# A routed expert layer behind cross attention: the list of surely positive units cut from 512 to 448 rows, the opening by head groups, and two inserted steps moved

## The chip, the cores and the metric

The kernel runs on one core of a Trainium2 chip. The metric is the device time of one execution in microseconds (us). TensorE (PE) multiplies, with its weight loads on a row of their own (PEld); VectorE (DVE) and ScalarE (ACT) do elementwise work; GpSimd (POOL) issues the indirect transfers; SyncE (SP) issues most of the others. In a profile, a wait is put down to whatever released it.

## The reference

```python
scores = scale * np.matmul(x, state.transpose(0, 1, 3, 2))      # x: 8 x 8 x 512 x 64, state: 8 x 8 x 32 x 64
a = softmax(scores);  xread = np.matmul(a, state)               # every token reads the states
a2 = softmax(scale * np.matmul(state, x.transpose(0, 1, 3, 2)))
sread = np.matmul(a2, x)                                        # every state reads the tokens
x = concat([xread, sread], axis=2) -> (8 * 544, 512)
expert_idx = argmax(x @ w_gate);  gate_w = softmax(...)[expert_idx]
out = gate_w * (relu(x @ w1[expert]) @ w2[expert])              # 8 experts, 512 -> 1024 -> 512, all float32
```

## The kernel before, in words

All 512 tokens of a batch go, as a rule, to one expert, which is guessed from the sum of the batch's states. A repair branch at the end computes anew every pair of batch and expert for which that does not hold, or whose lists overflowed; it is skipped when the count is zero.

Since `xread` is a weighted sum of states, the first layer of a batch is written `aT` (attention weights, 256 x 512 tokens) times `G` (states times w1, 256 x 1024 units). Each of the 1024 hidden units of a batch is put in one of three classes from mean and spread of its column of `G`: surely over zero for every token (then relu does nothing and the unit is linear), surely below zero (it is dropped), or unsure. `lists(b)` ranks them, and POOL scatters the columns to `g_dram`: rows 0 to `CAPP`-1 hold the sure ones, the next `CAPU` rows the unsure ones. `fetch(b)` reads the lists back, `gather(b, n)` gets the matching rows of w2 by indirect DMAs, one per block of 128 rows, and `mask(b)` zeroes unused rows.

`batch(b, insert)` then computes a batch from the lists. `pgu`: transposes of the unsure block. `pm`: for both halves g of the states, the sure rows times their rows of w2 (`NP` = 4 blocks of 128 rows, one matmul of 128x512 each), copied to `M` by ACT, so that the linear part needs only `aT` times `M`. `phu`: the unsure units, with relu, to `hu` (one block of 128 rows, one of 64). `py`: for each of 4 token blocks `aT` times `M` (two matmuls), the 128 unsure rows (one matmul), and the 64 last ones: two token blocks are done as a pair, each with a lhsT of 64 partitions, one on the lower and one on the upper half of the array. `store` scales by the gate and writes out. Batch 0 is done in full by `in_full`.

Everything for later batches is written into this work by hand. `batch` calls `insert()` 13 times: after `pgu`, four times during `pm`, after each of the two `phu`, and three times in each half of `py`. Each call takes the next entry of a plan, a string of letters; each letter runs the next step of a generator: T (`fronts`: transposes of x, scores, softmax), B (`backs`: five steps a batch, namely turn of the exponents a2, bound, state read, logits, `pcnt` = count of tokens by expert), S (`lists`), F (`fetch`, then two gathers), M (mask), R (`tokens`: sorting the 256 state rows by expert and three rounds of 128 rows through the experts' weights). Every engine executes its instructions in the order written here. PSUM tiles other than the scores come from one pool of 6 banks (`bank`).

An fp32 matmul of 128x512 stands in the trace as two records.

The opening: `load_x(0)` brings the 8 heads of batch 0 in two DMAs (heads 0 to 3, 4 to 7); `turn_x` transposes them, `scores` computes the scores of all heads in two groups (even and odd heads), `shifted`, `exp0`, `norm_read` and `turn_read` make the softmax for one group at a time, `turn_states` and `guess(1, B)` prepare states and experts of batches 1 to 7, and `states_w1` makes the first half of batch 0's `G`.

Of the kernel before, what the change touches and what calls it, by code (L numbers as in the profile page):

```python
# [20 lines left out]
def kernel(  # L21
# [52 lines left out]

    CAPP, CAPU = 512, 192
    YB = 4
    NP, NU = CAPP // 128, 2
    GW = 2 * 128 + 1
# [32 lines left out]
    def load_x(b, q):  # L111
        x_nat[b] = att.tile([128, H, NC, D], FP32, tag="x", bufs=2, name="x_nat")
        for h in (ts(0, 4), ts(1, 4)):
            q.dma_start(out=x_nat[b][:, h].rearrange("p h c d -> p h (c d)"),
                        in_=x[b, h].rearrange("h (p c) d -> p h (c d)", c=NC))

# [60 lines left out]
    nn = const.tile([128, B, 2], FP32)  # L177
    dve.memset(nn[:], 0.0)
    more = const.tile([128, NT], FP32)
# [90 lines left out]

    def scores(xT, st):

        for g in range(2):
            for q in range(4):
                for c in range(2):
                    pe.matmul(pa[ts(q, 32), c, g], lhsT=st[ts(c, 64), 2 * q + g, :], rhs=xT[ts(c, 64), 2 * q + g],
                              start=True, stop=True, skip_group_check=True)
# [26 lines left out]
    def new_aT():  # L304
        return ffn.tile([128, 2, NC, 4, 32], FP32, tag="aT", bufs=4, name="aT")
# [40 lines left out]
    def back(b):  # L346
# [25 lines left out]
        for g in range(2):  # L372
            for c in range(NC):
                for q in range(4):
                    pe.matmul(pw[ts(q, 32), g], lhsT=a2T[:, g, c, ts(q, 32)], rhs=x_nat[b][:, 2 * q + g, c, :],
                              start=(c == 0), stop=(c == NC - 1), skip_group_check=True)
# [113 lines left out]
    def store_batch(b):  # L490
        rows = out[ds(b * SO, S)].rearrange("(p c) f -> p c f", c=NC)

        def store(c, py):
            y = ffn.tile([128, DM], FP32, tag="y", bufs=YB, name="y")
            if b == B - 1 and c == NC - 1:
                dve.tensor_scalar(y[:], py[:], gw[:, NC * b + c, :], None, ALU.mult)
            else:
                act.activation(y[:], py[:], AF.Copy, scale=gw[:, NC * b + c, :])
            no_dep((act if b == B - 1 and c == NC - 2 else sp).dma_start(out=rows[:, c], in_=y[:]))
        return store  # L500
# [3 lines left out]
    def lists(b):  # L504
# [40 lines left out]
        dve.tensor_copy(out=nn[:, b], in_=pr[:, NFC:2 * NFC + 2:NFC + 1])  # L545
        fits, at_l, at_u, off_u = small("s_f"), small("s_l"), small("s_u"), small("s_o", 1)
        dve.scalar_tensor_tensor(fits[:], pr[:, 0:NFC], float(CAPP), lin, ALU.is_lt, ALU.mult)
        dve.scalar_tensor_tensor(at_l[:], pr[:, 0:NFC], -float(FAR), fits[:], ALU.add, ALU.mult)
        dve.tensor_scalar(off_u[:], nn[:, b, 0:1], -1.0, float(CAPP - FAR), ALU.mult, ALU.add)
        dve.scalar_tensor_tensor(at_u[:], pr[:, NFC + 1:2 * NFC + 1], off_u[:], und, ALU.add, ALU.mult)  # L550
# [11 lines left out]
    def fetch(b):  # L562

        t = gps[b] = ffn.tile([128, NP + NU, GW], FP32, tag="gp", bufs=2, name="gp")
        gp.dma_start(out=t[:, 0:NP + 1], in_=g_dram[0:CAPP + 128].rearrange("(j p) k -> p j k", p=128))
        for u in range(2):
            gp.dma_start(out=t[ts(u, 64), NP + 1], in_=g_dram[ds(CAPP + 128, 64)])
        w2cs[b] = []
# [11 lines left out]
    def mask(b):  # L580

        t = gps[b]
        mk = ffn.tile([128, NP + NU], FP32, tag="mk", bufs=2, name="mk")
        dve.tensor_scalar(mk[:, 0:NP], slot_p[:], nn[:, b, 0:1], None, ALU.is_lt)
        dve.scalar_tensor_tensor(mk[:, NP:], slot_u[:], nn[:, b, 0:1], nn[:, b, 1:2].to_broadcast([128, NU]),
                                 ALU.add, ALU.is_lt)
        for j in [NP, NP + 1, *range(NP)]:
            dve.tensor_scalar(t[:, j, 0:256], t[:, j, 0:256], mk[:, j:j + 1], None, ALU.mult)
# [3 lines left out]
    def batch(b, insert):  # L592
# [7 lines left out]
        insert()  # L600
        M = ffn.tile([128, 2, DM], FP32, tag="M", name="M")
        for g in range(2):
            pm = bank(name="pm")
            for j in range(NP):
                pe.matmul(pm[:], lhsT=t[:, j, ts(g, 128)], rhs=w2c[j][:], start=(j == 0), stop=(j == NP - 1))
                if j % 2:
                    insert()
            act.copy(M[:, g, :], pm[:])
        summed[0] = b
# [15 lines left out]
        for c0 in range(0, NC, 2):  # L625
            py = [bank(name="py") for _ in range(2)]
            for i in range(2):
                for g in range(2):
                    pe.matmul(py[i][:], lhsT=tokens_of(a)[:, g, ts(c0 + i, 128)], rhs=M[:, g, :],
                              start=(g == 0), stop=False)  # L630
                pe.matmul(py[i][:], lhsT=hu[0][:, ts(c0 + i, 128)], rhs=w2c[NP][:], start=False, stop=False)
                insert()
            for i in range(2):
                pe.matmul(py[i][:], lhsT=hu[1][ts(i, 64), ts(c0 // 2, 128)], rhs=w2c[NP + 1][ts(i, 64)],
                          start=False, stop=True)
            for i in range(2):
                store(c0 + i, py[i])
            insert()
# [159 lines left out]
    sx0 = new_sx()  # L798
    aTs[0] = new_aT()
    dve.tensor_copy(out=std[:, 0:2, 1], in_=std[:, 0:2, 0])  # L800
    turn_states(0, 2, copy_dve)
# [27 lines left out]
    off = const.tile([128, 1], FP32)  # L829
    gp.memset(off[:], -1.0 / NS)  # L830
    U128 = const.tile([128, 128], BF16)

# [3 lines left out]
    def late_constants():  # L836
        clear()
        yield
        dve.tensor_scalar(U128[:], colf[:], iota_p[:, 0:1], None, ALU.is_gt)
        tmp = const.tile([128, 1], FP32)  # L840
        quad = const.tile([128, 1], FP32)
        dve.tensor_scalar(quad[:], iota_p[:], 32.0, None, ALU.is_ge)
        for q in (64.0, 96.0):
            dve.scalar_tensor_tensor(quad[:], iota_p[:], q, quad[:], ALU.is_ge, ALU.add)
        dve.tensor_scalar(tmp[:], quad[:], float(SO - NS), iota_p[:, 0:1], ALU.mult, ALU.add)
        for t in range(NT):
            dve.tensor_scalar(tok_s[:, t:t + 1], tmp[:], float(4 * t * SO + S), None, ALU.add)
        dve.tensor_copy(out=slot_u[:, 0:1], in_=iota_p[:])
        dve.tensor_scalar(tmp[:], iota_p[:], 64.0, -64.0, ALU.is_ge, ALU.mult)
        dve.scalar_tensor_tensor(slot_u[:, 1:2], iota_p[:], 128.0, tmp[:], ALU.add, ALU.add)  # L850
        yield

# [83 lines left out]
    def count_left():  # L936
# [7 lines left out]
        tmp8 = const.tile([128, B], FP32)  # L944
        dve.tensor_tensor(tmp8[:], nn[:, :, 1], nn[:, :, 0], ALU.subtract)
        dve.tensor_scalar(over[:, :, 0], nn[:, :, 0], float(CAPP), None, ALU.is_gt)
        dve.scalar_tensor_tensor(over[:, :, 0], tmp8[:], float(CAPU), over[:, :, 0], ALU.is_gt, ALU.max)
        dve.tensor_tensor(others[:], others[:], over[:].to_broadcast([128, B, E]), ALU.max)
# [21 lines left out]
    with tc.If(number(rest_i[0:1, 0:1], B * E + NT * NR * 3) > 0):  # L970
# [4 lines left out]
        with tc.If(number(n_i[0:1, 0:1], B * E) > 0):  # L975
# [8 lines left out]
            with tc.For_i(0, n_pairs, 1):  # L984
# [20 lines left out]
                for h in range(H):  # L1005
                    sp.dma_start(out=xn[:, h].rearrange("p c d -> p (c d)"),
                                 in_=x[ds(bs, 1), h].rearrange("o (p c) d -> p (o c d)", c=NC))
# [69 lines left out]
```

## Time and profile before

| | us |
|---|---|
| median of 3 runs | 394.77 (393.68 to 395.79) |
| the profiled execution | 391.03 |
| its span, first to last instruction | 389.2 |
| PE busy in it | 359.8 (92%) |
| DVE, ACT, POOL busy | 189.5, 131.1, 123.3 |
| DMA | 92.65 MB, mean 238 GB/s |

Matmuls are pipelined and the ends of their records are modelled, so their starts say more than their durations: from start to start a record of 128x512 fp32 takes 0.43 us here.

### The profile page before, as it was taken

Reading aid. Unit: us, or ns where it says so; the run is one execution under the profiler, and the core shown is the slowest. Engines: PE = TensorE matmul, PEld = TensorE weight load, DVE = VectorE, ACT = ScalarE, POOL = GpSimd, SP = SyncE. Lnnn points to the kernel's source line nnn. Section 1 sums busy time; section 2 is a strip of 40 time slices with the busy share of each in tenths; the row PEclk is TensorE's granted clock in tenths of the full one; section 3 lists DMA queues with packets and bytes.
Section 4 is the critical chain, followed back from the end, with each engine's and each line's share of the span. In section 5 each row is a group of like instructions: output and inputs, shape, how many; then the busy total and the mean of one; then the engine's idle time right before and its main releaser. Section 6 shows DMA issues by size and latency. Waiting matters only on the chain. (4 is left out here: it accounts for less than half of the span.)

```text
span 389.2 us, 7854 instructions
## 1 busy us (share of the span) xinstructions
PE 359.8 (92%) x2660; PEld 166.3 (43%) x2660; DVE 189.5 (49%) x614; ACT 131.1 (34%) x249; POOL 123.3 (32%) x146
## 2 busy tenths in 40 slices
PE   5599999999799898999997799999999999999992
PEld 4344553645444364455441335333443443432330
DVE  3857678784588167967740223533733364000100
ACT  2464824623622444263334124104541032211010
POOL 2000017277317533643273321073510747000000
PEclk9899999999999899999998899999999999999997
DMA  7979992973563655243899999599996356979952
GB/s 167 376 235 278 242 365 84 318 231 106 159 195 109 196 158 178 96 133 82 281 367 334 346 395 390 198 322 262 329 331 207 128 161 199 314 238 340 389 200 85
DMA packets 50765, 92.65 MB, mean 238 GB/s; under 512 B 8007, under 2 KB 18258, under 8 KB 50720
## 3 DMA queue, kind: packets, MB, share of 16 engines
q1 hardware_dynamic: 41920, 69.95, 54.7%
q0 software_dynamic: 8128, 21.86, 17.9%
q8 instruction: 23, 0.38, 0.4%
q10 hardware_dynamic: 672, 0.28, 0.3%
q14 instruction: 22, 0.18, 0.1%
HBM read 83.40 MB, written 20.42 MB: 267 GB/s over the span
## 5 line engine op out<-in xcount | busy, mean ns | idle before, releaser
L51 POOL DMA_INDIRECT g_dram<-gt,to x56 | 56.9, 1016 | 132.2 <-DMA x_nat<-in_x_dram 52.9
L51 POOL DMA_INDIRECT w2c<-in_moe_w_dram,gp x42 | 44.0, 1048 | 58.3 <-DMA gp<-g_dram 31.4
L51 PE MATMUL py<-M,aT 128*128 128x512 f32 x112 | 54.2, 607 | 0.0
L51 PE MATMUL pm<-w2c,gp 128*128 128x512 f32 x112 | 53.1, 609 | 0.0
L51 PE MATMUL py<-w2c,hu 128*128 128x512 f32 (+1 forms) x112 | 44.7, 634 | 0.0
L51 ACT ACTIVATE y<-py,gw 128x512 f32<-128x512 f32 x31 | 20.0, 686 | 58.1 <-PE py L51 28.6
L51 PE MATMUL pgh<-s,sxT 128*32 128x512 f32 x192 | 28.3, 636 | 3.2 <-issue 2.8
L51 PEld LDWEIGHTS py<-M,aT 128*128 128x128 f32 x112 | 19.8, 189 | 26.7 <-issue 23.2
L51 DVE BATCH_NORM_STATS2 bn<-gt 128x6 f32<-128x256 f32 x56 | 20.2, 416 | 20.3 <-ACT gt L51 16.7
L51 PEld LDWEIGHTS pm<-w2c,gp 128*128 128x128 f32 x112 | 20.3, 195 | 20.8 <-issue 18.9
L51 DVE COPY G<-pG 128x512 f32<-128x512 f32 x14 | 9.6, 689 | 39.8 <-PE pG L51 23.8
L51 PEld LDWEIGHTS py<-w2c,hu 128*128 128x128 f32 (+1 forms) x112 | 15.1, 192 | 22.2 <-issue 22.1
L51 PE MATMUL pgy<-s,shT 128*32 128x512 f32 x192 | 23.7, 596 | 0.0
L51 PE MATMUL pG<-w1t,stT 64*32 64x512 f32 x256 | 21.2, 622 | 1.7 <-issue 1.6
L51 PE MATMUL py<-s,s 128*128 128x512 f32 x48 | 22.6, 603 | 0.0
L51 ACT COPY xT<-pxT 128x512 f32<-128x512 f32 x30 | 16.3, 604 | 15.5 <-PE pxT L51 13.1
L51 DVE COPY shT<-pth 128x512 f32<-128x512 f32 x3 | 2.1, 689 | 39.8 <-PE pth L51 39.8
L51 PE MATMUL phu<-aT,Gu 128*64 128x256 f32 (+1 forms) x84 | 20.7, 461 | 0.0
L51 ACT COPY gt<-pgt 128x512 f32<-128x512 f32 x28 | 15.9, 599 | 13.2 <-PE pgt L51 9.1
L51 POOL DMA_INDIRECT out_dram<-ys,xg x3 | 3.0, 991 | 52.2 <-DVE ys L51 49.5
L51 ACT ACTIVATE a<-pa,nm 128x512 f32<-128x512 f32 x16 | 10.9, 686 | 22.4 <-DVE nm L51 20.4
L51 PE MATMUL pxT<-ident,x_nat 128*128 128x128 f32 x128 | 17.8, 294 | 0.2 <-PE ph L51 0.2
(207 smaller groups left out, 487.2 us busy)
## 6 DMA issues: line engine op xcount, KB each, us to landing
s<-in_moe_w_dram SPq DMA_DIRECT2D x144, 256.0 KB
w1t<-in_moe_w_dram SPq DMA_DIRECT2D x7, 2048.0 KB
x_nat<-in_x_dram SPq DMA_DIRECT2D x16, 512.0 KB
out_dram<-y SPq DMA_DIRECT2D x31, 256.0 KB
gp<-g_dram POOLq DMA_DIRECT2D x7, 642.5 KB
ss_dram<-blank SPq DMA_DIRECT2D x8, 257.0 KB
w1t<-in_moe_w_dram SPq DMA_DIRECT2D x2, 1024.0 KB
s<-in_moe_w_dram SPq DMA_DIRECT2D x2, 768.0 KB
```

Of the source, the lines that this page charges most:

```text
L51: ins = getattr(self.engine, name)(*args, **kw)
```

## The change

`CAPP` goes from 512 to 448, so that the lists take 640 rows in place of 704. Sure units from rank 448 on are no longer dropped: the unsure list begins right behind row 447, and the surplus sure units are put there and treated as unsure. The fourth block of sure rows (384 to 447) is fetched twice, onto partitions 0 to 63 and 64 to 127, and its matmuls for g = 0 and g = 1 use one half of the array each. `fetch` issues four DMAs in place of three. Both `pm` banks are taken at once, and both copies to `M` come after the pair.

In `py`, the second half begins with its pair of 64-row matmuls and stores each block as it is done; the last block of the last batch is scaled half by ACT, half by DVE, and written by two DMAs on two queues.

`load_x` brings even heads first, then odd ones. In the opening, scores, shift and exponentials go group by group, the copy of the states and `turn_states` stand elsewhere, and `guess(1, B)` comes last. Two plan entries differ: the first B step of batch 3 (turn of exponents) moves from the last entry of batch 0 to the first of batch 1, and the `pcnt` of batch 4 from `BTR` to the entry behind it. The 13 calls of `insert` per batch stay; in `pm` they are three after 2, 4 and 6 matmuls and one after the pair and the copies.

```diff
-    CAPP, CAPU = 512, 192
+    CAPP, CAPU = 448, 192
-    NP, NU = CAPP // 128, 2
+    NP, NU = 4, 2
...
-        for h in (ts(0, 4), ts(1, 4)):
-            q.dma_start(out=x_nat[b][:, h].rearrange("p h c d -> p h (c d)"),
-                        in_=x[b, h].rearrange("h (p c) d -> p h (c d)", c=NC))
+        for g in range(2):
+            q.dma_start(out=x_nat[b][:, ts(g, 4)].rearrange("p h c d -> p h (c d)"),
+                        in_=x[b, g:H:2].rearrange("h (p c) d -> p h (c d)", c=NC))
...
             if b == B - 1 and c == NC - 1:
-                dve.tensor_scalar(y[:], py[:], gw[:, NC * b + c, :], None, ALU.mult)
+                act.activation(y[:, 0:256], py[:, 0:256], AF.Copy, scale=gw[:, NC * b + c, :])
+                dve.tensor_scalar(y[:, 256:], py[:, 256:], gw[:, NC * b + c, :], None, ALU.mult)
+                no_dep(act.dma_start(out=rows[:, c, 0:256], in_=y[:, 0:256]))
+                no_dep(sp.dma_start(out=rows[:, c, 256:], in_=y[:, 256:]))
             else:
                 act.activation(y[:], py[:], AF.Copy, scale=gw[:, NC * b + c, :])
-            no_dep((act if b == B - 1 and c == NC - 2 else sp).dma_start(out=rows[:, c], in_=y[:]))
+                no_dep(sp.dma_start(out=rows[:, c], in_=y[:]))
...
-        dve.scalar_tensor_tensor(fits[:], pr[:, 0:NFC], float(CAPP), lin, ALU.is_lt, ALU.mult)
-        dve.scalar_tensor_tensor(at_l[:], pr[:, 0:NFC], -float(FAR), fits[:], ALU.add, ALU.mult)
-        dve.tensor_scalar(off_u[:], nn[:, b, 0:1], -1.0, float(CAPP - FAR), ALU.mult, ALU.add)
+        dve.tensor_scalar(nl[:, b:b + 1], nn[:, b, 0:1], float(CAPP), None, ALU.min)
+        dve.scalar_tensor_tensor(at_l[:], pr[:, 0:NFC], -float(FAR), lin, ALU.add, ALU.mult)
+        dve.tensor_scalar(off_u[:], nl[:, b:b + 1], -1.0, float(CAPP - FAR), ALU.mult, ALU.add)
...
-        gp.dma_start(out=t[:, 0:NP + 1], in_=g_dram[0:CAPP + 128].rearrange("(j p) k -> p j k", p=128))
-        for u in range(2):
-            gp.dma_start(out=t[ts(u, 64), NP + 1], in_=g_dram[ds(CAPP + 128, 64)])
+        gp.dma_start(out=t[:, 0:NP - 1], in_=g_dram[0:384].rearrange("(j p) k -> p j k", p=128))
+        for i in range(2):
+            gp.dma_start(out=t[ts(i, 64), NP - 1::2], in_=g_dram[384:CAPP + CAPU].rearrange("(j p) k -> p j k", p=64)[:, 0::3])
+        gp.dma_start(out=t[:, NP], in_=g_dram[ds(CAPP, 128)])
...
+        pm = [bank(name="pm") for _ in range(2)]
+        for n in range(2 * NP - 2):
+            g, j = n // (NP - 1), n % (NP - 1)
+            pe.matmul(pm[g][:], lhsT=t[:, j, ts(g, 128)], rhs=w2c[j][:], start=(j == 0), stop=False, skip_group_check=True)
+            if n % 2:
+                insert()
         for g in range(2):
-            pm = bank(name="pm")
-            for j in range(NP):
-                pe.matmul(pm[:], lhsT=t[:, j, ts(g, 128)], rhs=w2c[j][:], start=(j == 0), stop=(j == NP - 1))
-                if j % 2:
-                    insert()
-            act.copy(M[:, g, :], pm[:])
+            pe.matmul(pm[g][:], lhsT=t[ts(g, 64), NP - 1, ts(g, 128)], rhs=w2c[NP - 1][ts(g, 64)], start=False, stop=True,
+                      skip_group_check=True)
+        for g in range(2):
+            act.copy(M[:, g, :], pm[g][:])
+        insert()
...
+            def few(start):
+                for i in range(2):
+                    pe.matmul(py[i][:], lhsT=hu[1][ts(i, 64), ts(c0 // 2, 128)], rhs=w2c[NP + 1][ts(i, 64)],
+                              start=start, stop=not start, skip_group_check=True)
+            if c0 > 0:
+                few(True)
...
+                if c0 > 0:
+                    store(c0 + i, py[i])
...
+    act.copy(std[:, 2:, 1], std[:, 2:, 0])
     exp0 = lambda g: act.activation(sx0[:, ts(g, 16)], sx0[:, ts(g, 16)], AF.Exp, bias=0.0, scale=SCALE)
-    scores(xT0, stT[:, 0])
-    shifted(sx0, [0])
-    exp0(0)
-    shifted(sx0, [1])
-    act.copy(std[:, 2:, 1], std[:, 2:, 0])
+    for g in range(2):
+        scores(xT0, stT[:, 0], [g])
+        shifted(sx0, [g])
+        exp0(g)
     turn_states(2, 6, act.copy)
-    turn_states(6, 10, act.copy)
     norm_read(sx0, [0])
-    exp0(1)
-    turn_states(10, 14, act.copy)
-    turn_states(14, 16, act.copy)
     turn_read(sx0, aTs[0], [0])
-    pick = guess(1, B)
-    norm_read(sx0, [1])
-    turn_read(sx0, aTs[0], [1])
...
     states_w1(w1t, stT[:, 0], G, 0, act.copy)
-    pick()
+    norm_read(sx0, [1])
+    turn_read(sx0, aTs[0], [1])
+    turn_states(6, 10, act.copy)
+    turn_states(10, 14, act.copy)
+    turn_states(14, 16, act.copy)
+    guess(1, B)()
...
-        "TGKK,TAT,A,TA,,TST,SBA,SSSS,BBTT,SSAT,TB,T,SBTS,TBST,BSSS,STBF,FSSB,,TT,B,T,,TTMS,SSBS"))
+        "TGKK,TAT,A,TA,,TST,SBA,SSSS,BBTT,SSAT,TB,T,SBTS,TBST,BSSS,STBF,FSSB,,TT,B,T,,TTMS,SSS"))
-        1: "FTFS,,,B,BT,SFBS,BTT,,,R,,MBSS,FSTB",
-        2: "STSS,TB,TF,RR,MFS,RFBS,BTR,,T,,R,TTS,SBTF",
+        1: "BFTFS,,,B,BT,SFBS,BTT,,,R,,MBSS,FSTB",
+        2: "STSS,TB,TF,RR,MFS,RFBS,TR,B,T,,R,TTS,SBTF",
```

More of the change, by code (lines that the diff above doesn't have):

```diff
@@ L177 @@
     nn = const.tile([128, B, 2], FP32)
-    dve.memset(nn[:], 0.0)
+    nl = const.tile([128, B], FP32)
+    for t in (nn, nl):
+        dve.memset(t[:], 0.0)
     more = const.tile([128, NT], FP32)
@@ L269, in new_xT, with scores @@
         return att.tile([128, H, 2, 128], FP32, tag="xt", name="xT")
-    def scores(xT, st):
-        for g in range(2):
+    def scores(xT, st, groups=(0, 1)):
+        for g in groups:
             for q in range(4):
                 for c in range(2):
-                    pe.matmul(pa[ts(q, 32), c, g], lhsT=st[ts(c, 64), 2 * q + g, :], rhs=xT[ts(c, 64), 2 * q + g],
+                    pe.matmul(pa[ts(q, 32), c, g], lhsT=st[ts(c, 64), 2 * q + g, :], rhs=xT[ts(c, 64), 4 * g + q],
                               start=True, stop=True, skip_group_check=True)
@@ L374, in back @@
                 for q in range(4):
-                    pe.matmul(pw[ts(q, 32), g], lhsT=a2T[:, g, c, ts(q, 32)], rhs=x_nat[b][:, 2 * q + g, c, :],
+                    pe.matmul(pw[ts(q, 32), g], lhsT=a2T[:, g, c, ts(q, 32)], rhs=x_nat[b][:, 4 * g + q, c, :],
                               start=(c == 0), stop=(c == NC - 1), skip_group_check=True)
@@ L545, in lists @@
         dve.tensor_copy(out=nn[:, b], in_=pr[:, NFC:2 * NFC + 2:NFC + 1])
-        fits, at_l, at_u, off_u = small("s_f"), small("s_l"), small("s_u"), small("s_o", 1)
-        dve.scalar_tensor_tensor(fits[:], pr[:, 0:NFC], float(CAPP), lin, ALU.is_lt, ALU.mult)
-        dve.scalar_tensor_tensor(at_l[:], pr[:, 0:NFC], -float(FAR), fits[:], ALU.add, ALU.mult)
-        dve.tensor_scalar(off_u[:], nn[:, b, 0:1], -1.0, float(CAPP - FAR), ALU.mult, ALU.add)
+        at_l, at_u, off_u = small("s_l"), small("s_u"), small("s_o", 1)
+        dve.tensor_scalar(nl[:, b:b + 1], nn[:, b, 0:1], float(CAPP), None, ALU.min)
+        dve.scalar_tensor_tensor(at_l[:], pr[:, 0:NFC], -float(FAR), lin, ALU.add, ALU.mult)
+        dve.tensor_scalar(off_u[:], nl[:, b:b + 1], -1.0, float(CAPP - FAR), ALU.mult, ALU.add)
         dve.scalar_tensor_tensor(at_u[:], pr[:, NFC + 1:2 * NFC + 1], off_u[:], und, ALU.add, ALU.mult)
@@ L584, in mask @@
         dve.tensor_scalar(mk[:, 0:NP], slot_p[:], nn[:, b, 0:1], None, ALU.is_lt)
-        dve.scalar_tensor_tensor(mk[:, NP:], slot_u[:], nn[:, b, 0:1], nn[:, b, 1:2].to_broadcast([128, NU]),
+        dve.scalar_tensor_tensor(mk[:, NP:], slot_u[:], nl[:, b:b + 1], nn[:, b, 1:2].to_broadcast([128, NU]),
                                  ALU.add, ALU.is_lt)
@@ L629, in batch @@
                     pe.matmul(py[i][:], lhsT=tokens_of(a)[:, g, ts(c0 + i, 128)], rhs=M[:, g, :],
-                              start=(g == 0), stop=False)
-                pe.matmul(py[i][:], lhsT=hu[0][:, ts(c0 + i, 128)], rhs=w2c[NP][:], start=False, stop=False)
-                insert()
[L633 to L637, printed above, removed]
+                              start=(c0 == 0 and g == 0), stop=False, skip_group_check=True)
+                pe.matmul(py[i][:], lhsT=hu[0][:, ts(c0 + i, 128)], rhs=w2c[NP][:], start=False, stop=c0 > 0,
+                          skip_group_check=True)
+                if c0 > 0:
+                    store(c0 + i, py[i])
+                insert()
+            if c0 == 0:
+                few(False)
+                for i in range(2):
+                    store(c0 + i, py[i])
             insert()
@@ L799 @@
     aTs[0] = new_aT()
+    off = const.tile([128, 1], FP32)
+    gp.memset(off[:], -1.0 / NS)
+    U128 = const.tile([128, 128], BF16)
     dve.tensor_copy(out=std[:, 0:2, 1], in_=std[:, 0:2, 0])
@@ L827 @@
     states_w1(w1t, stT[:, 0], G, 0, act.copy)
-    pick()
-    off = const.tile([128, 1], FP32)
-    gp.memset(off[:], -1.0 / NS)
-    U128 = const.tile([128, 128], BF16)
+    norm_read(sx0, [1])
[4 more added lines that the diff above has]
+    guess(1, B)()
     slot_u = const.tile([128, NU], FP32)
@@ L850, in late_constants @@
         dve.scalar_tensor_tensor(slot_u[:, 1:2], iota_p[:], 128.0, tmp[:], ALU.add, ALU.add)
+        dve.tensor_tensor(slot_p[:, NP - 1:NP], slot_p[:, NP - 1:NP], tmp[:], ALU.add)
         yield
@@ L944, in count_left @@
         tmp8 = const.tile([128, B], FP32)
-        dve.tensor_tensor(tmp8[:], nn[:, :, 1], nn[:, :, 0], ALU.subtract)
-        dve.tensor_scalar(over[:, :, 0], nn[:, :, 0], float(CAPP), None, ALU.is_gt)
-        dve.scalar_tensor_tensor(over[:, :, 0], tmp8[:], float(CAPU), over[:, :, 0], ALU.is_gt, ALU.max)
+        dve.tensor_tensor(tmp8[:], nn[:, :, 1], nl[:], ALU.subtract)
+        dve.tensor_scalar(over[:, :, 0], tmp8[:], float(CAPU), None, ALU.is_gt)
         dve.tensor_tensor(others[:], others[:], over[:].to_broadcast([128, B, E]), ALU.max)
@@ L1005 @@
                 for h in range(H):
-                    sp.dma_start(out=xn[:, h].rearrange("p c d -> p (c d)"),
+                    sp.dma_start(out=xn[:, h % 2 * 4 + h // 2].rearrange("p c d -> p (c d)"),
                                  in_=x[ds(bs, 1), h].rearrange("o (p c) d -> p (o c d)", c=NC))
```

## The prediction, on record before the changed kernel ran

> **What bounds the kernel now.** I read the page's busy times and slices first, then PE's matmuls in order of time, then the opening, SP's queue of the last third, and the places where PE stands still.
>
> ```profile
> PE 359.8 (92%) x2660; PEld 166.3 (43%) x2660; DVE 189.5 (49%) x614; ACT 131.1 (34%) x249; POOL 123.3 (32%) x146
> PE   5599999999799898999997799999999999999992
> PEclk9899999999999899999998899999999999999997
> ```
>
> PE is the bound nearly throughout; 389.2 - 359.8 leaves 29 us idle, and slices of 7 and 8 show where. So a matmul taken from PE's row shortens the run, except where something else is later. Batch 6 shows a `pm` with nothing inserted (timeline of PE; start, length):
>
> ```profile
> 311.42 1.13 PE L51 MATMUL py<-w2c,hu 64*128 64x512 f32 x4
> ...
> 313.43 7.11 PE L51 MATMUL pm<-w2c,gp 128*128 128x512 f32 x16
> 320.37 2.89 PE L51 MATMUL phu<-aT,Gu 128*128 128x512 f32 x12
> ```
>
> From start to start the 16 records take 6.94 us, 0.43 each. The pair of 64-row matmuls (311.42 to the next start at 312.48) takes 1.06 for four records: two run at a time, 2 x 0.43 plus 0.20 for changing the array's form.
>
> The opening (timeline, all engines):
>
> ```profile
> 9.94 0.69 DVE L51 COPY xT<-pxT 128x512 f32<-128x512 f32 x1 [1.01 <-PE pxT L51]
> ...
> 11.79 0.78 DVE L51 STREAM_TRANSPOSE sx<-pa 128x256 f32<-128x256 f32 x2 [1.16 <-PE pa L51]
> ...
> 14.59 0.92 ACT L51 COPY std<-std 128x896 f32<-128x896 f32 x1
> ...
> 15.56 2.22 PE L51 MATMUL pst<-ident,std 128*128 128x128 f32 x14 [3.82 <-ACT std L51]
> ...
> 20.54 0.71 DVE L51 STREAM_TRANSPOSE aT<-sx 128x512 f32<-128x512 f32 x1
> ...
> 21.27 1.98 PE L51 MATMUL ph<-aT,G 128*128 128x512 f32 x4 [0.15 <-ACT G L51]
> ```
>
> DVE's softmax chain runs without a break from 11.79 to 21.25 and releases batch 0's first `ph`; it starts only when all scores are there. PE idles 3.82 us for the copy of the states.
>
> The last third (SP's queue; two stretches: length, busy us of PE, PEld, DVE, ACT, POOL, clock, DMA share, GB/s):
>
> ```profile
> 324.65 0.33 SPq L51 DMA_DIRECT2D xg<-ss_dram  x1
> 326.60 14.18 SPq L51 DMA_DIRECT2D s<-in_moe_w_dram  x15
> 340.88 6.56 SPq L51 DMA_DIRECT2D out_dram<-y  x4
> 347.80 22.50 SPq L51 DMA_DIRECT2D s<-in_moe_w_dram  x33
> ```
>
> ```profile
> 336.00:368.00 32.00, 31.50 (x149) 10.79 (x147) 0.69 (x1) 6.04 (x11) 0.00 (x0) 1.00 0.92 318
> 382.10:389.20 7.10, 0.00 (x0) 0.00 (x0) 0.75 (x1) 0.69 (x1) 0.00 (x0) 0.73 0.21 77
> ```
>
> The third round of state rows needs 48 transfers of 256 KB, which run from 326.60 to about 375 back to back. PE's `pgh` and `pgy` starts are stretched by them: 5.65, 6.67 and 4.87 us for stretches that take 3.57 undisturbed. From 324.65 to 367.94 this stream is the clock, not PE. After the last matmul 7.1 us follow.
>
> Where PE stands still in between (timeline):
>
> ```profile
> 97.70 2.08 POOL L51 DMA_DIRECT2D gp<-g_dram  x3
> ...
> 99.30 0.59 ACT L51 COPY G<-pG 128x512 f32<-128x512 f32 x1 [2.33 <-remote]
> ...
> 99.94 0.66 PE L51 MATMUL pa<-ident,a 128*128 128x128 f32 x4 [2.19 <-ACT G L51]
> ```
>
> ```profile
> 155.21 0.26 PE L51 MATMUL pcnt<-oh,ones_b 128*128 128x8 bf16 x4 [1.31 <-DVE oh L51]
> ```
>
> The first is the turn of exponents that the change moves, the second the `pcnt`. In the first, `pG`'s matmuls started at 93.43 and ran about 1 us, yet ACT, idle from 96.98, began the copy at 99.30, in the middle of a train of POOL transfers. Similar stalls stand at 128.7 to 132.9, 204.5 to 207.4 and 217.8 to 221.9.
>
> **The change part by part.** *The pm cut.* Six matmuls and a pair: 12 x 0.43 + 1.06 = 6.22 in place of 6.94: 0.72 a batch. [...] In `py`, where the entry between the halves has no PE work (batches 1, 2, 3), the two pairs now touch: 0.20 less each. Batches 1 to 5: 5 x 0.72 + 3 x 0.20 = 4.2 us. Batches 6 and 7 lie before or in the weight stream; `xg` at 324.65 hangs on sorting that precedes batch 6's `pm`, so their 1.4 us become longer waits at `pgh`: nothing, at most 1.4.
>
> *The opening.* Scores of group 0 need only the first two copies of xT, so they run while DVE makes the fourth; DVE can start the chain at 9.94 + 0.69 = 10.63 in place of 11.79. The chain's operations stay the same and DVE is never idle in it: 1.1 us earlier at `ph`. Moved steps: ACT's copy of the states now comes before the exponentials (9.68 to 10.6, ACT is idle there; its DMA was issued at 2.31), `turn_states` 6 to 16 and `guess` come behind `states_w1`; their five ACT copies (0.55 or less each) and PE's 2 to 3 us must be done by 20.1. By the rows: exponentials end 15.6, one copy, G's two, three more, 18.6, `guess` and its sums 20.0: just covered, at most 0.5 late. `clear()` drops a DMA of SP's 6 (3.14 us), uncritical. Here the clock decides: from 13.0 to 16.43 PE was busy 0.87 us, and the next 3.41 us ran at a granted clock of 0.54, over small transposes. [...] If that falls on `ph` now, it costs up to 1.7. [...]
>
> *The two moved steps.* `pcnt` waits 1.31 for DVE; one entry later its `oh` is long done, and `prs`, now first, needs an `oh` that DVE finished at 153.37, before `phu` ends. Gain 1.4, from the whole gap behind `phu` (153.8 to 155.2); low end 0.5. The turn of exponents issues 8 transposes, two ACT copies (0.6), DVE's turn of aT (1.23) and ACT's square (1.15), no DMA; `Gu`'s copy and the third `pgt` now precede it. But that `pgt` needs the very G copies at 99.3 to 99.9, so the stall passes to it. I take 0; it may give 2.3.
>
> *The end.* y of 128x512 takes 0.75 on DVE; half width about 0.4 (ACT's 128x256 relu: 0.38). Two 256 KB stores land from 383.7 to 386.0; now the next to last goes out about 3 us sooner and 256 KB remain: about half. 0.35 + 0.65 = 1.0 us; ends 0.4 and 1.6.
>
> *What it adds.* A fourth fetch DMA per batch: 0.6 us of POOL (the short ones' length), 4.2 in all. Behind it stand gathers of w2; batch 7's end at 329.9 and `pm` starts at 336.9, so 7 us cover it. Two `pm` banks are held to the end of `pm`, so four of six circulate for inserted steps, not five: dense entries (batch 4: two `pG`, `pq`, `pw`, `pgt`) may wait for a copy of 0.6. Behind such an alloc stands all of PE. From 0 to 0.7 a batch for three dense batches; together with POOL I take 0.5, ends -0.5 (looser trains) and 4. M's copies are now both behind the pair, with about 3 us of `phu` ahead of their use: nothing. `lists` keeps its number of DVE operations: nothing.
>
> Sum: 4.2 + 1.1 + 1.4 + 1.0 - 0.5 = 7.2 us. Against the profiled execution: 391.03 - 7.2 = 383.8. It was 3.7 us under the median of the runs shown, so I carry the sum over: 394.77 - 7.2 = 387.6. Half a percent (2.0 us) is about what a measurement here can tell from no change.
>
> **The rivals.** *Stalls shrink too.* If shorter trains and the moved turn also take the 2.3 us at 97 and one of the 3 to 4 us stalls with its half-clock stretch, 5 more: 382.5. The rows show these stalls hinge on alignment, in either direction.
>
> *The gain is absorbed.* PE arrives sooner and waits for G copies or POOL's landings at the same absolute times. Only opening and end and little else count: 394.77 - 2.5 = 392.3. For it: POOL waits 31.4 us for fetches. Against: the trains start from PE's own results, so they move along.
>
> *Slower: a new stall in a dense batch.* One mechanism: with four banks circulating, PE stops in batch 4's entries behind a copy whose release comes late during a POOL train that is now 0.6 longer. Each such stop costs what the ones at 128.7 and 217.8 cost: about 3.8, plus 1.7 as the next 3.4 us run at 0.53 clock (132.5 to 135.9, 221.2 to 224.6). Two of them eat the gain (11 against 7.2); three give 394.77 - 7.2 + 16.5 = 404, two 398.6. It decides from the second on.
>
> *Not what it says.* If sure and unsure units of a batch exceed 640, the repair branch runs. Counted on the reference's inputs they are at most 608 (batch 3: 451 and 157), so I exclude it.
>
> **How the numbers follow.** Forecast 0.58 (387.6, its own range 384.5 to 391.5); stalls shrink 0.10 (382.5); absorbed 0.17 (392.3); slower 0.15 (398.6). Faster by over 0.5% (under 392.8): the first two and a little over a third of the third, 0.74. Within: 0.12, slower: 0.14. Leaving out the ends of the first rival and most of the last gives 382.5 to 395.0.
>
> **What would show it.** `pm` without insertions at 6.2 us from start to start; first `ph` near 20.1; no wait at the `pcnt` in batch 2's plan; a wait at the third `pgt` of batch 3's lists in place of the one at the turn; waits at `pgh` of the third round longer by about 1.4 us; 6 us behind the last matmul. Wrong: a `ph` under half clock, stops of PE in batch 4's `pm`, a later `xg`, more windows at half clock.

## The result, and the profile after

The changed kernel takes 393.59 us (median of 20 runs, 390.09 to 396.26), the kernel before 395.74 us (20 runs beside them): a ratio of 0.9958 with a 95% interval of 0.9934 to 0.9982. The ratio is of the executions outside a slower state that some fall into, the medians are of all, so 1.7 us by the ratio stands beside 2.2 by the medians. That is not 7.2: the direction holds, three quarters of the sum are missing. The profiled execution of the change is one above its median (395.17, span 393.3), that of before was one below its own (391.03), so the two traces are not subtracted end from end; they serve to see which step came out.

Some names that the lines use: `xg` is the DMA that fetches the 128 sorted state rows of a round, and the transfers of `s` behind it on SP's queue bring the weights ("the stream"). `pgh` (two halves) and `pgy` are the two layers of a round, `pth` the transposes between them. `pls` are the router's logits of the state rows, and `prs` is the first step of their sorting, which `xg` has to wait for.

The changed kernel's page, busy line and PE's slices:

```profile
PE 360.1 (92%) x2653; PEld 165.8 (42%) x2660; DVE 189.4 (48%) x615; ACT 132.2 (34%) x250; POOL 128.1 (33%) x153
PE   5699999999799699999988889999999969999992
```

PE's row is as busy as before although it has less to do. Slice by slice (9.8 us each): the one at 147 us, where `pcnt` waited, goes from 8 to 9; the one at 128 from 8 to 6, the one at 315 from 9 to 6, and the dip at 206 to 226 is now spread over 197 to 236. PE's timeline of the changed kernel (start, length; in brackets the wait before it and what ended it):

```profile
20.41 3.74 PE L51 MATMUL ph<-aT,G 128*128 128x512 f32 x4
...
100.45 0.70 PE L51 MATMUL pgt<-ident,G 128*128 128x128 f32 x4 [2.29 <-ACT G L51]
...
158.69 0.24 PE L51 MATMUL pcnt<-oh,ones_b 128*128 128x8 bf16 x4
...
230.98 1.05 PE L51 MATMUL pgh<-s,sxT 128*32 128x512 f32 x4 [0.48 <-DMA s<-in_moe_w_dram]
...
318.32 0.19 PE L51 MATMUL prs<-oh,U 128*128 128x8 bf16 x1 [3.30 <-DVE oh L51]
...
318.42 7.93 PE L51 MATMUL pm<-w2c,gp 128*128 128x512 f32 x16
```

Of the kernel before, the second `ph` and the second half of the first round's `pgh`:

```profile
25.47 1.98 PE L51 MATMUL ph<-aT,G 128*128 128x512 f32 x4
...
227.80 3.64 PE L51 MATMUL pgh<-s,sxT 128*32 128x512 f32 x32
```

`ph` starts 0.86 us sooner, but at half clock (granted 0.50 from 20.8 to 24.2 us; 3.74 in place of 1.98), and the second `ph` starts at 26.18, 0.71 us later than before. The stall passed from the turn of exponents to the third `pgt`, as forecast. `pcnt` waits no more. New are the last three: waits for weights in the first round of state rows (its second `pgh` half takes 8.42 us from start to start; it took 3.57), a wait of 3.30 at `prs`, and batch 6's `pm`, which was to take 6.2 us and takes 7.86, its first 3 us at half clock (granted 0.50 from 318.0 to 321.4). In SP's queue the third `xg` goes out at 328.43 (324.65 before) with a stream as long as before behind it; 7.2 us follow the last matmul, as before.

### The profile page after: what moved, and what is told of

It reads as the page before. It is cut to its first block, busy times and chain, and to the rows that moved or that the text cites. A ratio compares the mean times of both kernels' runs of the same rounds, so it can differ in the third digit from the quotient of the medians.

```text
span 393.3 us, 7852 instructions
## 1 busy us (share of the span) xinstructions
PE 360.1 (92%) x2653; PEld 165.8 (42%) x2660; DVE 189.4 (48%) x615; ACT 132.2 (34%) x250; POOL 128.1 (33%) x153
## 5 line engine op out<-in xcount | busy, mean ns | idle before, releaser
L51 POOL DMA_INDIRECT g_dram<-gt,to x56 | 58.0, 1036 | 143.7 <-DMA x_nat<-in_x_dram 53.6
L51 PE MATMUL pm<-w2c,gp 128*128 128x512 f32 (+1 forms) x112 | 48.5, 625 | 0.1
L51 ACT ACTIVATE y<-py,gw 128x512 f32<-128x512 f32 (+1 forms) x32 | 21.0, 680 | 81.4 <-issue 32.1
L51 PE MATMUL py<-w2c,hu 128*128 128x512 f32 (+1 forms) x112 | 42.6, 607 | 0.0
L51 PE MATMUL pgh<-s,sxT 128*32 128x512 f32 x192 | 32.0, 637 | 3.5 <-issue 2.5
L51 PEld LDWEIGHTS pm<-w2c,gp 128*128 128x128 f32 (+1 forms) x112 | 17.5, 194 | 19.3 <-issue 16.8
L51 PE MATMUL pgy<-s,shT 128*32 128x512 f32 x192 | 22.9, 595 | 0.0
L51 POOL DMA_DIRECT2D gp<-g_dram x28 | 18.5, 686 | 9.1 <-issue 5.5
L51 ACT COPY xT<-pxT 128x512 f32<-128x512 f32 x30 | 16.3, 601 | 11.1 <-PE pxT L51 9.2
L51 PE MATMUL pgt<-ident,G 128*128 128x128 f32 x112 | 16.5, 283 | 3.5 <-ACT G L51 3.4
L51 PE MATMUL pxT<-ident,x_nat 128*128 128x128 f32 x128 | 18.8, 304 | 0.0
```

What stands on the lines that cost most here:

```text
L51: ins = getattr(self.engine, name)(*args, **kw)
```

## The experiments

The kernel before ran beside each experiment on the same chip. The first four ran on a chip like that of the profiles above (before: 395.75 us). All others ran on chips where the same kernel before takes 372.9 to 376.0 us, without PE's stalls at 67, 97, 129 and 205 us.

**Parts of the change, each alone on the kernel before.** The pm cut (all that hangs on `CAPP`):

```diff
-    CAPP, CAPU = 512, 192
+    CAPP, CAPU = 448, 192
...
```

> The kernel before with the pm cut alone: 448 rows for sure units, the fourth fetch, the two banks of pm, the new lists; opening, moved steps and end stay as before. By the prediction's sum this alone is worth 4.2 - 0.5 = 3.7 us. The theory 'saved but lost later' (PE saves 0.72 us a batch, but in the stretch at 190 to 240 us and in the third round of weights the transfers are the clock) expects 1 to 1.5 us, with longer waits at pgh in both weight rounds. The rival 'new stalls from the moved steps' expects the whole 3.7 us here, since no step of the plans is moved.

394.13 us, ratio 0.9959 (0.9925 to 0.9994). The opening:

```diff
+    for g in range(2):
+        scores(xT0, stT[:, 0], [g])
+        shifted(sx0, [g])
+        exp0(g)
...
```

> The kernel before with the opening by head groups alone. By the prediction's sum 1.1 us faster. By the trace of the changed kernel, in which the first ph starts 0.86 us sooner but falls into a second stretch of half clock and is 1.35 us longer, this is worth nothing or costs up to 0.7 us.

393.58 us, 0.9947 (0.9911 to 0.9983). The two moved steps:

```diff
-        2: "STSS,TB,TF,RR,MFS,RFBS,BTR,,T,,R,TTS,SBTF",
+        2: "STSS,TB,TF,RR,MFS,RFBS,TR,B,T,,R,TTS,SBTF",
...
```

> The kernel before with the two moved steps alone (the plan of batch 2 with pcnt an entry later, the turn of exponents an entry later in batch 1's plan, the shorter last entry). By the prediction's sum 1.4 us faster, all of it from the pcnt; the turn of exponents gives nothing, as the stall passes to the third pgt. 'Saved but lost later' expects the 1.4 us at 156 and less than 0.7 us at the end, as the weights of round 0 at 190 to 240 us are the clock there.

397.25 us, 1.0002 (0.9952 to 1.0052). In its trace 4.33 us lie between `phu` and `prs` of that plan, 5.82 before: the 1.4 us of the forecast are there (1.49), and gone by the end. Order in `py` and last store:

```diff
+            if c0 > 0:
+                few(True)
...
+                no_dep(act.dma_start(out=rows[:, c, 0:256], in_=y[:, 0:256]))
+                no_dep(sp.dma_start(out=rows[:, c, 256:], in_=y[:, 256:]))
```

> The kernel before with the order in py (64-row pairs that touch) and the last store in two halves alone. By the prediction's sum 0.6 us from the touching pairs and 1.0 us from the end, 1.6 in all. By the trace of the changed kernel the end gives nothing (7.2 us behind the last matmul as before), so 0 to 0.6 us.

392.99 us, 0.9933 (0.9896 to 0.997). In its trace, of an execution of 399.45 us, 7.16 us lie behind the last matmul, so the gain is not the end's; and `prs` of batch 6 waits 3.13 us there, where the traces of the other three parts have at most 0.37. Four intervals of 0.3 to 0.5% to each side cannot share out 1.7 us: by the ratios the parts sum to 6.3 us, the whole gives 1.7. Inconclusive by time; they only say that the parts do not add up.

**Fewer weights.** Both kernels with two of the three transfers per piece in the rounds of state rows. This leaves out the third expert's weights; its matmuls stay and read the second's:

```diff
-    PLACE = (0, 0, 1, 2)
+    PLACE = (0, 0, 1, 1)
...
-                    for q in range(3):
+                    for q in range(2):
```

> The kernel before with two of the three weight transfers per piece in the rounds of state rows; the third expert's part is left out of the transfers, its matmuls stay. If the weight streams are the clock of the rounds, this is several us faster than before (3 to 10).

> The changed kernel with two of the three weight transfers per piece, left out in the same way as in its partner. 'Saved but lost later' expects the gap between the two to widen from 1.7 to between 4 and 6 us once the streams no longer set the time. The rival 'new stalls from the moved steps' expects the gap to stay near 1.7 us.

365.37 and 359.94 us (before on that chip: 372.91): 5.4 us apart. With a third of the stream gone most of the forecast gain is there. In the traces the changed kernel is ahead by 3.84 us at the last `pgh` of the first round. But the edit also takes away a third of the register tests that SP makes for these transfers (see below): the first `xg` follows SP's load of the registers by 12.7 us in e5, by 16.7 in e9 with all of them. So this pair alone does not part the stream from SP's work.

**Filler matmuls in the opening's gaps**, to keep the clock up:

```diff
+        if g == 0:
+            filler(1)
...
+    filler(2)
```

> The changed kernel with filler matmuls (transposes of a row tile into a bank nobody reads) in three gaps of PE's opening. If half clock eats the opening's gain, the stretch from 17.37 to 24.2 us runs at full clock and the kernel is 1.7 to 2.5 us faster than the changed one; if the clock there is not what counts, it is the same or up to 1 us slower for the added matmuls.

**The R steps of batch 6 put behind the F steps:**

```diff
-        6: "RFR,,,,F,,F,,R,M,,,R",
+        6: "F,,RR,,F,,F,,R,M,,,R",
```

> The changed kernel with batch 6's R steps put back behind the F steps, so that prs stands behind four matmuls of pm and no longer waits 3.47 us. The rival 'new stalls from the moved steps' expects 4 to 5 us less than the changed kernel (the wait and the half clock after it). 'Saved but lost later' expects the wait of PE gone and the time the same within 1 us, as the third round's stream starts when xg is issued and ends when it ends.

374.15 and 376.65 us on the same chip (before: 372.91). The first shows no half clock (mean granted clock 0.996), with `ph` at 20.92 in place of 19.08 in its neighbour, and has `phu` of batch 1 still 0.55 later. The filler costs as much (1.84 us at `ph`) as the full clock gives back, so it does not tell what the half clock costs. The second removes the wait of `prs` and is 2.5 us slower than its neighbour: `prs` comes 2.27 us later, the third `xg` 1.96, the last matmul 2.70. The changed kernel itself was not on this chip, so only the two are compared, and they differ by the filler as well; neither theory expected this. Here the time of `prs`, and of what it releases, counted for more than a wait of PE.

**Both kernels as they are, on one chip without the stalls.**

> The kernel before, unchanged, for a trace of it on the same chip as the next three. Every theory expects a ratio of 1.000 with an interval that shows how small a difference can be told.

> The changed kernel, unchanged, on the same chip. On a chip where the engines' semaphores come late behind POOL's trains (stalls of PE at 67, 97, 130 and 205 us) every theory expects 1 to 3 us less than before; on a chip without these stalls 'SP and the streams are the clock' expects a difference between -1 and +2 us, since PE's saving up to the first gather of state rows ends in waits for weights.

373.93 us, 0.9988 (0.9958 to 1.0018), and 373.34 us, 0.9985 (0.9955 to 1.0015): here the change does nothing that can be told. These two traces agree to hundredths where nothing differs, so they show where the time goes (start of the same matmul, us):

```
                                before    changed   difference
first ph                         21.22      19.93     -1.29
phu of batch 1                  108.17     106.36     -1.81
prs in batch 2                  147.95     144.41     -3.54
phu of batch 3                  178.62     174.38     -4.24
first xg issued                 177.72     175.53     -2.19
first pgh of the first round    196.34     191.69     -4.65
last pgh of the first round     218.43     219.01     +0.58
last pgy of the second round    289.10     288.11     -1.00
prs in batch 6                  298.74     298.72     -0.02
phu of batch 6                  305.75     306.84     +1.09
last matmul ends                364.10     363.80     -0.30
```

PE's timeline in the first round, kernel before:

```profile
196.34 3.82 PE L51 MATMUL pgh<-s,sxT 128*32 128x512 f32 x32
...
210.07 6.29 PE L51 MATMUL pgh<-s,sxT 128*32 128x512 f32 x28
```

and the changed kernel:

```profile
191.69 4.67 PE L51 MATMUL pgh<-s,sxT 128*32 128x512 f32 x32
...
210.12 5.43 PE L51 MATMUL pgh<-s,sxT 128*32 128x512 f32 x12 [2.78 <-DMA s<-in_moe_w_dram]
215.84 3.77 PE L51 MATMUL pgh<-s,sxT 128*32 128x512 f32 x12 [0.29 <-DMA s<-in_moe_w_dram]
```

PE comes 4.65 us sooner and leaves 0.58 later. A half takes 3.57 undisturbed; the two take 3.75 and 8.88 before, 4.60 and 13.26 after. The DMA share from 178 to 220 us is 1.01 to 1.04 in both. From `xg` to the end of the second half 41.2 us pass before, 44.0 after, and on the first chip 43.9 and 44.3: it gets no shorter when PE comes sooner.

What fills the longer stretch stands in the DMA rows for it. From `xg` to the end of the second half the hardware queue that SP's transfers use moves 11.7 MB in both traces, and POOL's queue 3.03 MB before and 3.74 after. Its gathers of w2 follow PE and now fall into the stretch. With the tests and the full weights, all six traces of the changed kernel have these 3.74 MB and take 43.8 to 44.4 us (the three of the kernel before: 2.96 to 3.22 MB, 41.2 to 43.9 us). e7 ran it at full clock and took 43.8 too, so the half clock that e10 has there from 210.0 to 213.4 is not the cause. POOL's share was seen, not varied.

**Why the stream starts so late.** `xg` is issued 30 us after `prs`. SP's queue shows nothing there but stores that seem to wait; between them its trace has 192 instructions that the page does not count. They stand behind the load of the experts' registers (161.06) and last, with the second round's load and two stores, until `w1t` and `xg` at 177.2: for each of the 96 weight transfers of two rounds SP tests that the condition's register is at most 1, since its range was declared as 0 to 7. Declaring the range takes the tests away, and with them 48 of the third round:

```diff
             ex[r] = values_of(eg[t][0:1, r].rearrange("p a q -> p (a q)"), SP)
+            ex[r] = list(ex[r][0:3]) + [nc.s_assert_within(v, min_val=0, max_val=1, skip_runtime_bounds_check_because="0 or 1")
+                                        for v in ex[r][3:]]
```

> The kernel before, without the check that SP makes on the condition's register ahead of each weight transfer of the state rounds (96 pairs of instructions behind the first register load, about 12 us of SP, and 48 pairs in the third round). The new theory 'SP's register work and the weight stream behind it are the clock from about 160 to 235 us' expects the first xg about 10 us sooner and the kernel 3 to 8 us faster. The rival 'the late semaphores and the moved steps are the loss' expects no change over 1 us.

> The changed kernel without the same checks. The new theory expects it faster by as much as its partner and by part of the hidden saving on top: 3 to 6 us below the kernel before without checks. The rival expects the gap between the two to stay what it is with the checks.

367.33 us, 0.9809 (0.9784 to 0.9833), and 364.00 us, 0.9747 (0.9708 to 0.9787). SP's queue of before with the tests:

```profile
177.72 0.50 SPq L51 DMA_DIRECT2D xg<-ss_dram  x1
178.83 14.68 SPq L51 DMA_DIRECT2D s<-in_moe_w_dram  x15
```

and of the changed kernel without them (with them its `xg` goes out at 175.53):

```profile
162.76 0.33 SPq L51 DMA_DIRECT2D xg<-ss_dram  x1
164.38 17.69 SPq L51 DMA_DIRECT2D s<-in_moe_w_dram  x15
```

The DMA share from 160 to 176 us rises from 0.42 to 0.79 in the kernel before and from 0.47 to 0.94 in the changed one, and every `pgh` half of the first round takes 3.57 or 3.62. In the traces with tests PE was 4.65 us ahead at the first `pgh` and 0.30 at the end of the last matmul; without them it is 5.51 ahead (e11 to e12) and still 5.24. By time the two kernels without tests are 3.3 us apart by the medians, 2.3 by the ratios, whose intervals just touch; those with tests were 0.6 and 0.1 apart. The theory that the saving is made and then waits for SP and the stream holds on this chip; the rival, that the moved steps alone eat it, falls for the first 190 us.

Two things bear on the size. The third round's tests go too: from its `xg` to its last transfer 44.1 us pass with them and 42.7 without (e9, e11), so up to 1.4 us of the gain may be theirs. And behind the last matmul 8.4 to 8.7 us pass in all five traces without tests, in place of 7.1 to 7.2; why was not tried.

**The wait at `prs`.** In the table the changed kernel loses 1.0 us before `prs` of batch 6 and 1.1 behind it. PE's timeline of the changed kernel:

```profile
298.72 0.19 PE L51 MATMUL prs<-oh,U 128*128 128x8 bf16 x1 [0.76 <-DVE oh L51]
...
298.83 8.08 PE L51 MATMUL pm<-w2c,gp 128*128 128x512 f32 x16
```

The pair of 64-row matmuls (1.06 us) stood between the router's `pls` and `prs` and covered DVE's work. The new order in `py` puts it ahead of `pls`; PE waits, and the granted clock is 0.50 from 298.7 to 302.1. Put back in batch 5 alone:

```diff
-            if c0 > 0:
+            late = c0 == 0 or b == 5
+            if not late:
                 few(True)
...
-            if c0 == 0:
+            if late:
                 few(False)
```

on the change without tests (e13 beside its partner e16), and on the plain change (e17):

> The changed kernel without SP's checks, and with the 64-row pairs of batch 5 put back behind the halves of py, so that one pair lies again between the router's matmuls and prs. If the wait at prs is lost time, the wait of 0.93 us goes, prs and the third xg come about 1 us sooner, and the kernel is 0.5 to 1.5 us faster than its partner without this; the rival (the third stream hides it, or the pair costs the same elsewhere) expects a difference within 0.5 us.

> The changed kernel without SP's checks once more, as the partner of e13 on the same chip. About 2.5% under the kernel before, as in its first run, whatever the theory of the rest.

> The changed kernel, SP's checks in place, with only the 64-row pairs of batch 5 put back behind the halves of py. If the wait at prs and the half clock behind it are lost time, the phu after it starts about 2 us sooner than in the changed kernel, and the kernel is 1 to 2 us faster than it (0.4 to 0.8% under the kernel before on a chip without the late semaphores). If the third weight stream hides it, the time is the changed kernel's within 0.5 us.

e13 takes 362.05 us, e16 364.42, with ratios of 0.9623 (0.9581 to 0.9664) and 0.9729 (0.9672 to 0.9785) to the kernel before (375.97). e17 takes 372.31 us, 0.9966 (0.993 to 1.0002), and its timeline has no wait and full clock:

```profile
297.46 0.17 PE L51 MATMUL prs<-oh,U 128*128 128x8 bf16 x1
...
297.52 6.46 PE L51 MATMUL pm<-w2c,gp 128*128 128x512 f32 x16
```

Against the plain change (e10) it has `pgh` of the first round at the same 191.69, `prs` 1.26 us sooner, `phu` of batch 6 2.94, the third `xg` 1.53, the last matmul 1.14. Of these 0.29 are there already at the last `pgy` of the second round, ahead of the pair. So the wait is real time for PE, about 2.6 us, but in these two traces the third stream lets 0.9 through, and by time e17 (0.9966) cannot be told from e10 (0.9985). Without the tests e13 and e16 can: 2.4 us apart by the medians. Half clock stood right behind `prs` in five of six traces with that wait off the first chip (e6, e10, e12, e15, e16; not e7), and in none of those without it.

**The end.** Both kernels without the branch for leftovers and the repair work behind it, which these inputs never need:

```diff
-    with tc.If(number(rest_i[0:1, 0:1], B * E + NT * NR * 3) > 0):
...
```

> The kernel before without the branch for leftovers, which these inputs never take; the repair work behind it is left out. If SP's branch is the bound behind the last matmul, the end shrinks from 7.2 to about 6 us, when the last 256 KB stores have landed 3.9 us after it and the closing semaphores follow; if the stores are the bound, it stays within 0.5 us.

> The changed kernel without the same branch, which leaves out the repair work. If SP's branch is the bound behind the last matmul, the end shrinks from 7.2 to about 4.5 to 5 us here, 1 us or more below its partner's, as the halved last store lands 2.5 us after the last matmul; if it is not, both ends stay near 7.2.

373.11 us, 0.993 (0.9895 to 0.9964), and 371.66 us, 0.9884 (0.9843 to 0.9925). SP's instructions, us behind the end of the last matmul:

```
                         last store   branch    next instruction   end of the span
e9  before                  0.91       1.66          4.95              7.22
e10 changed                 1.11       1.93          4.86              7.13
e14 before, no branch       0.91         -           1.29              4.85
e15 changed, no branch      1.11         -           1.49              4.25
```

The end of before shrinks from 7.22 to 4.85 us, where about 6 was expected. With the branch about 3 us pass behind it whatever the stores do, and the halved store gives 0.1. In the changed kernel's first trace two packets of instruction fetch (8 KB each) fall into that gap, 2.7 and 3.2 us behind the last matmul; whether SP waits for them there was not shown. Without the branch the halved store gives 0.6, less than the 1.0 forecast, as the two halves of y are scaled one after the other (DVE begins at 0.59, when ACT is done at 0.56).

**The fastest version once more.**

> The changed kernel without SP's checks and with the pairs of batch 5 put back, once more: 3 to 4% under the kernel before, as in its first run; on a chip with the late semaphores, where PE is later at the first weights, the checks hide more and it should gain less, 1.5 to 3%.

360.76 us beside 373.90 of before, 0.9628 (0.9586 to 0.9669). It repeats at 3.7 to 3.8%. It did not fall on a chip with the stalls at 67, 97, 129 and 205 us, so that part of the expectation stays untried.

## Why the prediction was wrong, point by point

- **The pm cut: right in kind, 0.58 in place of 0.72.** From the first `pm` to `phu` the seven batches are shorter by 0.62, 0.77, 0.55, 0.51, 0.51, 0.56, 0.56 (e9 to e10, for batch 4 e11 to e12, for batch 6 e9 to e17). A `pm` without insertions takes 6.39, not 6.22. The row that I took (0.20, a pair's surplus) was too small, as it begins with the pair: in the changed kernel's trace the record ahead of the pair in batch 6 takes 0.52 from start to start (324.70 to 325.22) in place of 0.43. The other 0.08 that the sum left out are the first record's, behind `prs`: 0.50 in the trace of before (313.43 to 313.93).
- **The opening: right where the clock spared it, wrong where the prediction was made.** `ph` comes 1.29 us sooner in e10, forecast 1.1. But in 9 of the 12 traces with the new opening (all but e7, e10 and e17) half clock covers the first `ph`; in all eight with the old one it ends before it. On the first chip that puts the second `ph` 0.71 us later, close to the -0.6 that the forecast's 1.1 less the 1.7 of a `ph` at half clock gives; the prediction took 1.1.
- **The two moved steps: right on PE.** 1.39 us between `phu` of batch 2 and `prs` (−2.15 to −3.54), forecast 1.4; the stall of the turn passed on as said. But the experts' registers, which SP waits for, come only 2.2 us sooner (158.84 against 161.06). DVE reads `prs` behind a softmax, 5.5 us after it in e9 and 6.5 in e10 (153.47 and 150.92), so most of the 1.4 us is lost there; and its four operations behind the later `pcnt` now stand inside the sorting.
- **What it adds: right in size by luck.** One new wait of 0.56 us of PE ahead of 126.56 in e10 (for ACT's copy of G); 0.5 was taken, for POOL and the banks. In e9 the pair of 64-row matmuls stands at that place and PE does not wait, so the order in `py` is the likelier cause; it was not tried.
- **The step that failed: carrying the sum to the end.** "From 324.65 to 367.94 this stream is the clock, not PE" was taken for the only such stretch. The first round, 190 to 231 us in that very profile, is a second one: DMA share 1.02 to 1.05 there, and the last `pgh` half just did not wait. I took the missing wait for slack. So on the chip of e9 and e10 4.65 us that PE had saved by then, and which the prediction put at about 5 (1.1 + 3 x 0.72 + 1.4 + 0.4 for two batches' pairs), came to nothing: 0.58 us late at the end of the round. The argument against the absorbed rival, "the trains start from PE's own results, so they move along", overlooked the 16.7 us that SP spends between the load of its registers and the stream.
- **Batches 4 and 5: right in the sum.** 1.58 us between the two rounds, forecast 1.44; the two cuts of `pm` are 1.02 of it.
- **The order in `py`: half seen.** The touching pairs were counted as 0.20 each, and so they are (161.54 to 163.46 in the changed kernel's trace, 1.92 for the two in place of twice 1.06); that the pair had covered DVE's work ahead of batch 6's `prs` was not. It costs about 2.6 us of PE with the half clock, 0.9 at the end.
- **The end: wrong, 0.1 for 1.0.** The landing was taken for the bound; it is SP's branch.
- **The rivals.** "Absorbed" (392.3, at 0.17) came nearest to the outcome, in part by luck: it held PE up at copies of G and POOL's landings, not at SP's tests and the stream, and it counted the end in full. The slower one, stops in batch 4 for want of banks, did not appear: batch 4's `pm` has no such wait.

Shown by experiments: the tests and the first stream (e5, e6, e9 to e12), the pair (e13, e16, e17), the end (e14, e15), all on chips without the stalls; on the one where both kernels ran as they are (e9, e10) the change gains nothing that can be told. Only argued: that the same ledger holds on the first chip, where the 1.7 us were measured. Its two traces show the longer second half of `pgh` and the wait at `prs`, but no saving ahead of the first round: PE is 2.03 us later at `phu` of batch 2 and 0.22 later at the first `pgh` (207.67 against 207.45). There the opening and the stalls, which move by 1 to 2 us from kernel to kernel, had taken it already in these two executions, which are 4.1 us apart. How much of the missing sum is due to which stays open, and so does why that chip has the stalls.

## What to carry to other kernels

A stretch in which the DMA engines are full can be a clock of its own even when PE hardly waits in it (178 to 220 us of e9: a DMA share of 1.01 to 1.03, 0.57 us of PE's waits for weights; in e10 PE came 4.65 us sooner and left 0.58 later): sum the savings stage by stage, and stop the sum at each such stretch. Follow what starts the stream back to its issuing engine, and count the instructions there that the profile leaves out of its busy times (here 192 ahead of the first round, 0.12 us a pair). Before a small piece of work is moved, look at what its neighbours wait for: it may be the cover of a wait (here 1.06 us of PE ahead of `prs`).

## What the runs showed of the hardware

- The same program takes 395.7 us on one chip and 372.9 to 376.0 on four others. On the first, PE waits at 67, 97, 129 and 205 us (0.95, 2.19, 1.22 and 2.76 us in the profile of before), each time in or just behind a train of transfers that POOL issues; at 97 and 205 us ACT's copies start late as well (after 2.33 and 2.67 us idle). On the others these four waits are missing. At the first `pgh` the traces are 11.1 us apart, at the last matmul 17.9.
- A register test on SP is two instructions and took 0.12 us, from one pair's start to the next; without the 96 of them the first `xg` went out 10.2 us sooner (167.54 against 177.72 in the kernel before).
- Two short waits of PE, 0.86 and 0.76 us within 3 us (at `pls` and `prs` in e10), were followed by half clock for 3.41 us in five of six traces, at a cost of about 1.6 us in `pm` (8.01 against 6.39). In e10 PE's row was busy for 1.81 of the 3.41 us before it.
